# The first sequence of a convolution and mixture-of-experts kernel, convolved in blocks of 112 consecutive tokens by TensorE with tap matrices

## The chip, the cores and the metric

The kernel runs on one core of a Trainium2 chip. The metric is the device time of one launch in microseconds (us); each time quoted is the median of the runs of a kernel, and each figure from a trace is of its one profiled execution.

PE is TensorE's matmuls, PEld its weight loads, DVE VectorE, ACT ScalarE, POOL GpSimd, SP the queue that issues most loads. In a profile line, `L207` is a line of that kernel's source, and the line numbers shift between kernels: the output scaling on DVE is L772 in the kernel before and L862 in the changed one, the convolution step L207 and L346.

## The reference, cut to what matters

```python
# lightweight convolution: x (8, 3584, 192), 8 heads of 24 channels, 7 taps, causal
w = exp(w - max(w)); w = w / (sum(w) + 1e-9)
out[b, s, h*24:(h+1)*24] = sum_k w[h, k] * x_pad[b, s + k, h*24:(h+1)*24]
# mixture of experts on that: 8 experts of 192 -> 1024 -> 192
for b in range(B):
    prev_e = -1
    for s in range(S):
        fresh_e = argmax(logits[b, s])
        e = fresh_e if s == 0 or local_gate[b, s] < 0.5 else prev_e   # locality gate
        prev_e = e
        out[b, s] = softmax(logits[b, s])[e] * (relu(x[b, s] @ w1[e]) @ w2[e])
```

Each token's expert may depend on the token before it, so the router (the step that picks a token's expert) is a scan along the sequence.

## The kernel before

The tokens are worked in 16 groups of 1792 (two per sequence). A group is convolved, its logits and its router give every token a slot of its expert, POOL scatters the rows to these slots, and blocks of 128 or 256 full slots go through the experts. The first 35 blocks have one unit of 128 rows, then come 87 of two units and 20 of one. Blocks 0 to 6 need rows of group 0 alone, 7 (0-based) and on also those of group 1, 21 and on those of group 2; the first three of two units, 35 to 37, need group 3, and 38 and on group 4. Output scalings are counted below in units from 0: units 0 to 34 are the blocks 0 to 34, and unit 37 is the first of block 36. Groups 0 and 1 are sequence 0: nothing can hide them, as no expert has a row yet.

In the kernel before, a partition holds 14 consecutive tokens, and the load has 128 rows:

```python
def load_x(g):
    x_sb = xs.tile([P, NX, D], F32, name="x_sb")           # 128 x (14 + 6) x 192
    win = bass.AP(tensor=src.tensor, offset=..., ap=[[NT * D, P], [1, NX * D]])
    nc.sync.dma_start(out=x_sb.rearrange("p t d -> p (t d)"), in_=win)
```

Four of group 0's heads go to PE with diagonal matrices, seven matmuls each; the other four to DVE, one first tap and six steps each. From group 2 on all eight heads are on DVE, 48 steps per group, with the first taps on ACT:

```python
for k in range(1, KC):
    nc.vector.scalar_tensor_tensor(cols(h), chans(h, k), c[:, h, k:k + 1],
                                   cols(h), Alu.mult, Alu.add)
    yield 0.6
```

Once experts run, each block lets DVE do a quota of that work, measured in rough microseconds, ahead of the scaling of its own output:

```python
for i, (_, n, _, _) in enumerate(blocks):
    ensure(i)                          # rows; waits until the group of a block is routed
    weights(i + AHEAD)
    hT = hidden(n, wbs[i], xT)
    ...
    step(2.5 if n == 1 else 4.2)
    output(n, wbs.pop(i), xgs.pop(i), hT)      # calls step(1.2) ahead of its scaling on DVE
    step(1.3 if n == 1 else 3.0)
```

With 0.6 charged per convolution step, a one-unit block does 10 of them. The order of instructions on each engine is that of the program (no scheduler moves them).

## Time and profile before

| | before |
|---|---|
| first timing, median (range) | 1382.17 us (1381.35 to 1384.19, 3 runs) |
| the profiled execution | 1367.91 us, span of the core 1366.1 |
| PE busy, share of the span | 97% |
| first expert matmul | 71.64 us |
| output scaling of block 1 on DVE | 88.02 us |
| pace of blocks 1 to 34 | 6.17 us |

The second line is 14 us below the first.

The busy line of the page gives, per engine, busy us, share of the span and instructions; the slices give the share of each fortieth (34 us) in tenths:

```profile
PE 1327.2 (97%) x17142; PEld 1252.3 (92%) x17142; DVE 795.1 (58%) x2459; ACT 512.1 (37%) x1146; POOL 481.2 (35%) x513
...
PE   6789999999999999999999999999999999999998
```

PE is full but for the first three slices. What a change of the first sequence can win lies there. How to read the rest is shown in the prediction below: windows first (which stage has an engine that is not full), then the timeline of that stage (which instruction waits for what).

### The profile page before, as it was taken

What the parts mean: (1) busy time and instruction counts of PE and PEld (TensorE: products, weight loads), DVE (VectorE), ACT (ScalarE), POOL (GpSimd) and SP (SyncE); (2) the same over time, 40 slices, a digit from 0 to 9 for tenths busy, and PEclk for the clock granted to TensorE, in tenths of its full rate; (3) what the DMA queues carried; (4) which work ended last, traced back from release to release, by engine and by line L of the source; (5) the groups of instructions that cost most, each with busy time, mean ns of one, the idle gap of its engine ahead of it and who ended that gap; (6) DMA issues with size and microseconds to landing.
All of it is one profiled execution on the core that took longest, in us unless ns stands there. A gap on an engine that the chain in (4) does not pass through costs nothing. (4 is left out here: it accounts for less than half of the span.)

```text
span 1366.1 us, 41871 instructions
## 1 busy us (share of the span) xinstructions
PE 1327.2 (97%) x17142; PEld 1252.3 (92%) x17142; DVE 795.1 (58%) x2459; ACT 512.1 (37%) x1146; POOL 481.2 (35%) x513
## 2 busy tenths in 40 slices
PE   6789999999999999999999999999999999999998
PEld 4488999999999999999999999999999999999997
DVE  6778999988878777878686868684500000000000
ACT  3243444434333333333343434333333333333333
POOL 1442444434343434344444344443343111112111
PEclk9989999999999999999999999999999999999999
DMA  4399999996675757676767676565566555556893
GB/s 181 102 375 374 374 390 373 359 353 251 235 273 206 267 208 265 213 264 219 264 228 265 223 266 220 208 211 208 212 221 224 202 196 181 181 178 235 318 325 131
DMA packets 65812, 340.75 MB, mean 249 GB/s; under 512 B 12369, under 2 KB 23240, under 8 KB 45395
## 3 DMA queue, kind: packets, MB, share of 16 engines
q1 hardware_dynamic: 43488, 285.35, 57.8%
q0 software_dynamic: 22128, 52.70, 10.2%
q8 instruction: 136, 2.23, 0.7%
q14 instruction: 58, 0.47, 0.1%
q10 hardware_dynamic: 2, 0.00, 0.0%
HBM read 285.20 MB, written 53.29 MB: 248 GB/s over the span
## 5 line engine op out<-in xcount | busy, mean ns | idle before, releaser
L760 PE MATMUL yps<-wb,hT 64*128 64x192 f32 x7328 | 636.9, 325 | 3.7 <-DVE o_sb L772 2.0
L744 PE MATMUL hps<-xT,wb 64*128 64x256 f32 (+1 forms) x6816 | 630.4, 337 | 0.8 <-ACT xT L730 0.6
L760 PEld LDWEIGHTS yps<-wb,hT 64*128 64x128 f32 x7328 | 599.7, 187 | 8.5 <-issue 4.5
L744 PEld LDWEIGHTS hps<-xT,wb 64*128 64x128 f32 x6816 | 567.1, 188 | 41.5 <-issue 1.1
L776 POOL DMA_INDIRECT out_dram<-o_sb,xg x229 | 231.5, 1011 | 664.3 <-DVE o_sb L772 591.6
L207 DVE SCALAR_TENSOR_TENSOR y_sb<-x_sb,c,y_sb 128x336 f32<-128x336 f32 x720 | 406.2, 573 | 28.5 <-ACT y_sb L182 9.3
L749 ACT ACTIVATE hT<-hps 128x512 f32<-128x512 f32 (+1 forms) x568 | 261.3, 512 | 361.2 <-PE hps L744 361.0
L772 DVE SCALAR_TENSOR_TENSOR o_sb<-yps,xg,o_sb 128x192 f32<-128x192 f32 x229 | 87.2, 412 | 488.6 <-ACT o_sb L768 488.6
L567 POOL DMA_INDIRECT slots<-y_sb,posi x224 | 222.7, 994 | 185.7 <-ACT hT L749 92.2
L768 ACT ACTIVATE o_sb<-yps,xg 128x192 f32<-128x192 f32 x229 | 87.0, 419 | 420.6 <-PE yps L760 417.0
L730 ACT COPY xT<-xps 128x768 f32<-128x768 f32 (+1 forms) x142 | 96.7, 681 | 11.6 <-PE xps L279 11.6
L279 PEld LDWEIGHTS xps<-ident,xg 64*128 64x128 f32 x1374 | 71.2, 140 | 13.8 <-issue 3.9
L279 PE MATMUL xps<-ident,xg 64*128 64x64 f32 x1374 | 72.5, 222 | 5.8 <-DMA xg<-slots 5.8
L182 ACT ACTIVATE y_sb<-x_sb,c 128x336 f32<-128x336 f32 x116 | 66.7, 586 | 0.0
L341 DVE STREAM_TRANSPOSE z<-y_sb 128x768 f32<-128x768 f32 (+1 forms) x56 | 45.5, 853 | 0.5
L367 DVE COPY lt<-lq 32x36 f32<-32x36 f32 x224 | 41.6, 186 | 3.5
L351 PE MATMUL hps<-z,wg 64*32 64x128 f32 x1344 | 26.7, 274 | 1.4 <-DVE z L341 1.3
L351 PEld LDWEIGHTS hps<-z,wg 64*32 64x32 f32 x1344 | 20.7, 105 | 5.0 <-DVE z L341 3.0
L190 PE MATMUL hps<-x_sb,wb 128*128 128x336 f32 x56 | 18.9, 506 | 4.0 <-DMA x_sb<-in_x_dram 4.0
L190 PEld LDWEIGHTS hps<-x_sb,wb 128*128 128x128 f32 x56 | 12.1, 218 | 10.5 <-issue 6.2
L190 PE MATMUL yps<-x_sb,wb 128*128 128x336 f32 x56 | 16.8, 451 | 0.0
L190 PEld LDWEIGHTS yps<-x_sb,wb 128*128 128x128 f32 x56 | 10.3, 190 | 4.5
(165 smaller groups left out, 336.0 us busy)
## 6 DMA issues: line engine op xcount, KB each, us to landing
wb<-in_w_dram SPq DMA_DIRECT2D x142, 1536.0 KB
x_sb<-in_x_dram SPq DMA_DIRECT2D x16, 1920.0 KB
xg<-slots SPq DMA_DIRECT2D x87, 258.0 KB
xg<-slots SPq DMA_DIRECT2D x55, 129.0 KB
out_dram<-o_sb,xg POOLq DMA_INDIRECT x229
slots<-y_sb,posi POOLq DMA_INDIRECT x224
wg<-in_wgl_dram SPq DMA_DIRECT2D x1, 144.0 KB
slots<-pad SPq DMA_DIRECT2D x1, 129.0 KB
```

Of the source, the lines that this page charges most:

```text
L182: nc.scalar.activation(cols(h), chans(h, 0), Act.Copy, scale=c[:, h, 0:1])
L190: nc.tensor.matmul(acc, lhsT=dg_of(i, k), rhs=chans(h, k), start=(k == 0), stop=(k == KC - 1))
L207: nc.vector.scalar_tensor_tensor(cols(h), chans(h, k), c[:, h, k:k + 1], cols(h), Alu.mult, Alu.add)
L279: nc.tensor.transpose(to, src[rows], identity=ident[rows, rows])
L567: ins = nc.gpsimd.indirect_dma_start(out=slots[:, :], in_=rows, in_offset=None, out_offset=bass.IndirectOffsetOnAxis(ap=to, axis=0)).ins
L730: copied = nc.scalar.copy(to, at)
L744: nc.tensor.matmul(hps[half][:, j, w], lhsT=wb[rows, f0:f0 + P], rhs=xT[rows, d, w], start=(d == 0 and j == 0), stop=(d == KD - 1), skip_g ...
L749: relu = nc.scalar.activation(hT[:, m:m + 2, w], hps[half][:, :, w], Act.Relu)
L760: nc.tensor.matmul(yps[half][:, k * D:(k + 1) * D], lhsT=hT[rows, m, k * P:(k + 1) * P], rhs=wb[rows, WA + m * D:WA + (m + 1) * D], start= ...
L768: nc.scalar.activation(o_sb[:, k, :], y[k][0], Act.Copy, scale=xg[:, k, 0:1])
L772: nc.vector.scalar_tensor_tensor(o_sb[:, k, :], y[k][1], xg[:, k, 0:1], o_sb[:, k, :], Alu.mult, Alu.add)
L776: sent = nc.gpsimd.indirect_dma_start(out=out, in_=o_sb[:, k, :], in_offset=None, out_offset=bass.IndirectOffsetOnAxis(ap=xg.bitcast(I32)[ ...
```

## The change

Its intent: each group of sequence 0 becomes 16 blocks of 112 consecutive tokens, a token per partition, with the six tokens before them: 118 rows. One matmul then convolves one head of eight blocks with a banded matrix of taps (118 x 112), 16 matmuls per group in place of 28 matmuls and 28 DVE operations in group 0, and the loads are contiguous. The logits are computed from these blocks, and the router's scan runs along 16 rows. Because sequence 0 then needs little of DVE, the change also brings work forward, ahead of the first expert block: ten scatters of group 1 in place of four, and `step(15)`, convolution steps of group 2.

```diff
+NB = 16
+TB = PT // NB            # 112 tokens
+NI = TB + HALO           # 118 rows
+NH = NB // 2
@@ loads @@
+    def load_b(g):
+        x_sb = xs.tile([P, NX, D], F32, name="x_sb")
+        xv = x_sb.rearrange("p t d -> p (t d)")[:NI, :NB * D].rearrange("p (b d) -> p b d", d=D)
+        for b in (slice(0, NH), slice(NH, NB)):
+            nc.sync.dma_start(out=xv[:, b, :], in_=xb[g, :, b, :])
+        return xv
...
-        x_in = {0: load_x(0)}
+        nc.scalar.dma_start(out=hank[:NI], in_=wh)
+        x_in = {0: load_b(0)}
...
+        x_in[1] = load_b(1)
@@ convolution of sequence 0 @@
-    for gen in reversed(conv(0, x_in.pop(0), ON_PE, True)):
-        for _ in gen:
-            pass
+    def wide_conv(g, xv, y_sb, yr, both):
+        for b0 in (0, NH):
+            for h in range(H):
+                ps = hps_p.tile([P, 512], F32, name="hps")[:TB, :NH * GS]
+                nc.tensor.matmul(ps, lhsT=hank[:NI, h, :],
+                                 rhs=xv[:, b0:b0 + NH, h * GS:(h + 1) * GS],
+                                 start=True, stop=True)
...                             # leaves through ACT, in group 0 through DVE in turn
@@ order of the first sequence @@
+    conv1 = wide_conv(1, x_in.pop(1), yb, rest(zb), False)
+    for i, _ in enumerate(wide_route(0, ya, acc[0])):
+        for _ in range([6, 5, 5, 0][i]):
+            next(conv1, None)
...
+    for _ in wide_route(1, yb, acc[1]):
+        step(1.2)
+    for _ in range(10):
+        put()
+    step(15)
```

Not shown: the logits and the router of the first sequence (`wide_logits`, `wide_route`), whose parts the prediction counts, and the host's layouts of x and of the taps, which copy and fill but do no arithmetic.

## The prediction

> **What bounds the kernel now.** I read the table of busy time by windows first, to see in which stage TensorE (PE) is not full:
>
> ```profile
> 0.00:70.00 70.00, 47.81 (x280) 30.14 (x280) 49.97 (x159) 21.57 (x53) 20.03 (x52) 0.94 0.39 140
> 100.00:200.00 100.00, 95.67 (x1590) 92.98 (x1588) 92.45 (x295) 42.23 (x118) 38.10 (x38) 1.00 0.98 380
> 600.00:800.00 200.00, 200.00 (x2524) 188.87 (x2522) 153.10 (x470) 77.86 (x159) 81.88 (x81) 1.00 0.68 243
> ```
>
> Columns: window, length, busy us of PE, weight loads, VectorE (DVE), ScalarE (ACT), GpSimd (POOL), PE clock, DMA share, GB/s. From 400 us on PE is always busy: it is the bound, and the change leaves it alone. The change lives in the first 70 us, a chain before any expert runs. The timeline gives its links:
>
> ```profile
> 8.56 0.40 DVE L180 TENSOR_SCALAR y_sb<-x_sb,c 128x336 f32<-128x336 f32 x1 [2.04 <-DMA x_sb<-in_x_dram]
> ...
> 36.53 0.27 DVE L377 TENSOR_REDUCE mx<-lt 128x14 f32<-128x112 f32 x1
> ...
> 46.56 0.17 DVE L539 CAST posi<-pos 128x14 int32<-128x14 f32 x1
> ...
> 47.67 1.27 POOL L567 DMA_INDIRECT slots<-y_sb,posi  x1 [18.58 <-issue]
> ...
> 64.61 0.96 POOL L567 DMA_INDIRECT slots<-y_sb,posi  x1 [0.30 <-issue]
> ...
> 68.41 1.19 SPq L697 DMA_DIRECT2D xg<-slots  x2
> ...
> 71.64 4.79 PEld L744 LDWEIGHTS hps<-xT,wb 64*128 64x128 f32 x48 [0.76 <-ACT xT L730]
> ```
>
> So: group 0's x at 8.6, logits at 36.5, slots at 46.7, 14 scatters on POOL (one per 1.27 us) to 65.6, rows back, first expert matmul at 71.64. A second bound follows. DVE's timeline once experts run:
>
> ```profile
> 88.02 0.42 DVE L772 SCALAR_TENSOR_TENSOR o_sb<-yps,xg,o_sb 128x192 f32<-128x192 f32 x1 [1.88 <-ACT o_sb L768]
> 88.36 5.84 DVE L207 SCALAR_TENSOR_TENSOR y_sb<-x_sb,c,y_sb 128x336 f32<-128x336 f32 x10
> 94.12 0.41 DVE L772 SCALAR_TENSOR_TENSOR o_sb<-yps,xg,o_sb 128x192 f32<-128x192 f32 x1
> ```
>
> Each one-unit block queues ten convolution steps (5.8 us) and one output scaling (0.4 us) on DVE: 6.1 us. PE needs 5.51 us (its timeline has L744 starting at 87.37 and 92.89). From block 1's L772 (88.02) to block 34's (291.72) it is 203.7 us, 6.17 per block: DVE paces the 35 one-unit blocks. Afterwards two-unit blocks come every 10.8 us on PE. So what counts is **when DVE reaches block 1's scaling**.
>
> **What the Trainium skill says.** (1) "DMA: Bandwidth & Descriptors", section "Why a DMA increments its semaphore by 16 and not by 1": a transfer issued from SP or ACT uses the largest number of DMA engines, up to 16, that divides the outer dimension; 128 partitions get 16, 100 get 10, 127 one. The trace before cannot confirm it: its large loads all have 128 partitions (423 GB/s in 5 to 10 us, so an estimated 26.4 GB/s per engine). (2) "Trainium Kernel Development and Optimization", "Key Constraints": the SP and ACT queues share the same 16 engines. Not shown here either. (3) "TensorE: Matmul & The Clock Gate", Part 1: PE starts at half rate until it has been busy some microseconds. The trace agrees: the convolution's first passes start every 0.56 us up to 14.4 us, then the timeline merges 45 passes into 12.67 us, 0.28 each. (4) Same page, "Step-by-step": matmuls stay in program order. Relevant because the change puts group 1's matmuls ahead of group 0's router on PE.
>
> **The change, part by part.**
>
> *Loads.* Before: 128 rows of 15,360 B (1.97 MB). After: 118 rows (112 tokens and 6 of halo), two transfers of 0.725 MB per group, and tap matrices of 118 rows (0.423 MB) on ACT's queue. 118 = 2 x 59, so by (1) every one of them runs on **two engines, the same two**: 52.9 GB/s instead of 423. From about 2 us (the small weight load landed at 2.05): taps and group 0's x, 1.87 MB, take 35.4 us, to 37; group 1's halves land at 51 and 65. Were they on 16 engines, x of group 0 would be there at about 7.
>
> *Convolution.* Removed: 28 matmuls (18.9 us), 24 DVE steps and 4 first taps (15.9 us), 28 diagonal builds. Added: 16 matmuls of 192 columns. At 0.56 us per cold pass of 336 columns, a pass of 192 costs 0.32, a matmul (two passes) 0.64 cold, 0.32 warm; leaving through ACT and DVE in turn at 0.42 (as L768, same width) hides beside that. With x at hand this stage would end at 17 instead of 28. With x at 37 only the second half's eight remain, to 42.3.
>
> *Logits, router.* 24 transposes, six evictions of 448 columns (0.5 to 0.6), products of 1.5 per half, a turn back: I sum 7.3 us against 8.3 before. Logits at 49.7. Router: 1.9 to the change flags, then a turn and scans on 16 rows (2.9), then counts on PE. But PE's order has eleven of group 1's convolution matmuls before the counting matmuls, and the ninth needs group 1's second half: 65. Three cold ones (1.9) and the counts (0.9): 67.6. DVE's last eight operations (2.6): slots at 70.2 against 46.7.
>
> *Scatters.* 16 of 112 rows, not 14 of 128: POOL ends 2 x 1.27 later relative to its start. First at 71.1, last over at 91.5; plus the 6.07 from there to the expert matmul in the trace before: **97.6 against 71.6**.
>
> *DVE ahead of the experts.* Group 1's convolution leaves through ACT alone, done at 72; its logits at 80.3; its router with eight convolution steps of group 2 and the table: 17.5, so 98. The instruction order then puts **33 convolution steps** (18.9) before block 0's scaling, which ends at 117.4; seven more and two transposes (5.9): block 1's scaling starts at 123.2, against 88.02, +35.2. PE needs only 105 for block 0, so DVE decides.
>
> *Given back.* By instruction order DVE is then exactly four blocks ahead: each later block carries the same load as block i+4 did before. But as each block still gets its ten steps, the pace stays 6.1 and the lead buys nothing. Before has one bad interval (blocks 5 to 6, 113.67 to 122.08, 8.4 us, PE waiting for rows of group 1); after would not: -2.3. Four ordinary blocks (24.6) in place of 25.65: -1. Sum: 35.2 - 3.3 = **+32**, about 1414.
>
> **Rivals.**
> A. *The loads do use all engines.* Then slots 0 come at 35.7, first expert matmul at 62.5, nine earlier. The router of group 1 with its table ends at 63 on DVE; 33 steps follow, block 0's scaling ends at 82.3, block 1's starts at 88.5, against 88.02. The nine microseconds vanish in DVE's queue; the -3.3 remains: some 1379. For it: a tuned kernel would hardly keep a load that waits 30 us; against it: the page's rule, given with examples. 15 in 100.
> B. *The early DVE work pays fully* (lead becomes pace, blocks at 5.51 us): up to 33 x 0.6 = 20 us back. Against it: the load per block in the instruction order is unchanged up to block 35. It would make 1394 with two-engine loads.
> C. *Clock.* PE idles through the loads, so more matmuls run cold; 2 to 4 us more in group 1's logits, on DVE's path: 1418. For it: the clock column shows 0.50 in 65 to 75 before, after a sparse stretch.
>
> **Range and chances.** Main line 1414, plus or minus 8; rival A at 1379, 15 in 100. I put the time at 1412, a little below the main line for B, and the range from 1380 to 1424, to hold most of A's weight. The 2% limits are 1354.5 and 1409.8: faster 0.01, same 0.38, slower 0.61. (The profiled run before was 1367.91 us against the timed 1382.17; I take the difference as constant.)
>
> **What would show it.** DMA share in the first 35 us near 2/16, about 50 GB/s, instead of 181; PE waiting for x_sb from in_xb_dram until about 37, and within the router until about 65; first scatter at 71, first expert matmul at 97, block 0's output scaling at 117 behind 33 convolution steps; then blocks 6.1 to 6.2 us apart and the same PE-bound stage. The prediction is wrong if x lands before 10 us (then rival A, and the first scatter at 36), if the scatters of 112 rows differ much from 0.96 us, or if the one-unit blocks run at 5.5 us after the lead.

## The result, and the profile after

The changed kernel takes 1435.68 us (median of 4, 1434.69 to 1437.28), the kernel before on the same chip 1381.99 (4 runs). The ratio is 1.0387, 95% interval 1.0369 to 1.0405: slower by nearly 4%. The direction is as predicted; the time lies 12 us above the predicted range and 24 above the predicted value.

The table of busy time by windows, changed kernel. Columns as in the prediction: window, length, busy us of PE, PEld, DVE, ACT, POOL, PE clock, DMA share, GB/s:

```profile
0.00:10.00 10.00, 0.56 (x2) 0.49 (x2) 0.67 (x4) 1.49 (x2) 4.35 (x39) 1.00 0.17 51
10.00:20.00 10.00, 0.00 (x0) 0.00 (x0) 0.00 (x0) 0.00 (x0) 0.00 (x0) 1.00 0.13 53
20.00:30.00 10.00, 0.00 (x0) 0.00 (x0) 0.00 (x0) 1.76 (x7) 0.00 (x0) 1.00 0.13 52
...
50.00:60.00 10.00, 7.25 (x35) 5.34 (x33) 5.74 (x24) 3.31 (x9) 0.00 (x0) 0.83 0.72 214
60.00:70.00 10.00, 0.22 (x2) 0.09 (x1) 0.62 (x4) 1.76 (x4) 0.00 (x0) 0.61 0.13 54
```

All engines stand still from 10 to 28 us and again from 62 to 70, while the DMA engines are busy by 0.13, that is 2 of 16 (0.125), at 52 to 54 GB/s. Between 50 and 60 another load, x of group 2 with 128 rows, runs beside them: 214 GB/s in all. The timelines of PE, then of DVE (start, busy us, engine, line, operation, out<-in, count, and in brackets the wait with its releaser):

```profile
32.27 5.46 PE L179 MATMUL hps<-x_sb,wb 118*112 118x192 f32 x16
39.70 5.43 PE L179 MATMUL hps<-x_sb,wb 118*112 118x192 f32 x16 [1.96 <-DMA x_sb<-in_xb_dram]
...
69.94 2.23 PE L179 MATMUL hps<-x_sb,wb 118*112 118x192 f32 x6 [9.78 <-DMA x_sb<-in_xb_dram]
...
102.03 5.12 PE L834 MATMUL hps<-xT,wb 64*128 64x128 f32 x48 [0.58 <-ACT xT L820]
```

```profile
75.64 0.17 DVE L435 CAST posi<-pos 112x16 int32<-112x16 f32 x1
...
86.82 0.39 DVE L240 COPY wb<-yps 128x224 f32<-128x224 f32 x1 [6.79 <-remote]
90.34 0.31 DVE L245 COPY lt<-yps 112x144 f32<-112x144 f32 x1 [3.13 <-issue]
...
109.37 19.36 DVE L346 SCALAR_TENSOR_TENSOR y_sb<-x_sb,c,y_sb 128x336 f32<-128x336 f32 x33
128.65 0.41 DVE L862 SCALAR_TENSOR_TENSOR o_sb<-yps,xg,o_sb 128x192 f32<-128x192 f32 x1
...
136.10 0.38 DVE L862 SCALAR_TENSOR_TENSOR o_sb<-yps,xg,o_sb 128x192 f32<-128x192 f32 x1
```

The chain is the predicted one. Group 0's second half comes at 39.7; the convolution of group 1 waits for its second half to 69.9 in the middle of group 0's router; the slots are there at 75.6; DVE then ends the router of group 1 at 109.4 and does 33 convolution steps in a row before the first output scaling at 128.65. The two lines at 86.82 and 90.34 were not foreseen: DVE waits 6.8 us for something "remote" and then 3.1 us in a wait marked "issue". These are the profile's words for a wait that ended on a signal to which it finds no instruction, and for a wait in which it sees nothing waited for.

### The profile page after: what moved, and what is told of

It reads as the page before. It is cut to its first block, busy times and chain, and to the rows that moved or that the text cites. A ratio compares the mean times of both kernels' runs of the same rounds, so it can differ in the third digit from the quotient of the medians.

```text
span 1435.6 us, 41650 instructions
## 1 busy us (share of the span) xinstructions
PE 1344.5 (94%) x17048; PEld 1298.1 (90%) x17048; DVE 777.2 (54%) x2420; ACT 515.1 (36%) x1145; POOL 484.8 (34%) x522
## 5 line engine op out<-in xcount | busy, mean ns | idle before, releaser
L834 PE MATMUL hps<-xT,wb 64*128 64x256 f32 (+1 forms) x6816 | 653.6, 340 | 11.5 <-issue 10.0
L850 PE MATMUL yps<-wb,hT 64*128 64x192 f32 x7328 | 649.9, 326 | 6.8 <-issue 2.7
L834 PEld LDWEIGHTS hps<-xT,wb 64*128 64x128 f32 x6816 | 612.8, 190 | 30.1 <-issue 17.8
L850 PEld LDWEIGHTS yps<-wb,hT 64*128 64x128 f32 x7328 | 609.7, 188 | 13.9 <-issue 6.4
L346 DVE SCALAR_TENSOR_TENSOR y_sb<-x_sb,c,y_sb 128x336 f32<-128x336 f32 x672 | 382.5, 580 | 52.5 <-ACT y_sb L338 22.2
L318 PEld LDWEIGHTS xps<-ident,xg 64*128 64x128 f32 x1374 | 81.4, 140 | 3.6 <-DMA xg<-slots 0.3
L318 PE MATMUL xps<-ident,xg 64*128 64x64 f32 x1374 | 80.4, 223 | 0.0
L338 ACT ACTIVATE y_sb<-x_sb,c 128x336 f32<-128x336 f32 x112 | 62.4, 583 | 0.0
L179 PE MATMUL hps<-x_sb,wb 118*112 118x192 f32 x64 | 21.1, 514 | 11.7 <-DMA x_sb<-in_xb_dram 11.7
L179 PEld LDWEIGHTS hps<-x_sb,wb 118*112 118x112 f32 x64 | 18.1, 294 | 13.5 <-issue 12.5
```

Of the source, the lines that this page charges most:

```text
L318: nc.tensor.transpose(to, src[rows], identity=ident[rows, rows])
L338: nc.scalar.activation(cols(h), chans(h, 0), Act.Copy, scale=c[:, h, 0:1])
L834: nc.tensor.matmul(hps[half][:, j, w], lhsT=wb[rows, f0:f0 + P], rhs=xT[rows, d, w], start=(d == 0 and j == 0), stop=(d == KD - 1), skip_g ...
L850: nc.tensor.matmul(yps[half][:, k * D:(k + 1) * D], lhsT=hT[rows, m, k * P:(k + 1) * P], rhs=wb[rows, WA + m * D:WA + (m + 1) * D], start= ...
```

## The experiments

Eighteen runs, in six calls; runs of one call share a chip and its runs of the kernel before. The table sorts them by chip. "Before" is its median there; the difference is of medians.

| run | chip | before | this | difference | ratio (95% interval) |
|---|---|---|---|---|---|
| e0_before | 0 | 1382.66 | 1382.72 | +0.1 | 1.0000 (0.9976 to 1.0025) |
| e1_pad128 | 0 | 1382.66 | 1399.25 | +16.6 | 1.0127 (1.0087 to 1.0166) |
| e3_nostep | 0 | 1382.66 | 1422.45 | +39.8 | 1.0281 (1.0256 to 1.0306) |
| e4_before_two | 0 | 1382.66 | 1416.26 | +33.6 | 1.0239 (1.0213 to 1.0266) |
| e22_pad_short | 0 | 1382.35 | 1388.96 | +6.6 | 1.0047 (1.0035 to 1.0060) |
| e2_pad_nostep | 12 | 1366.61 | 1361.22 | -5.4 | 0.9954 (0.9940 to 0.9967) |
| e7_split | 12 | 1366.61 | 1370.15 | +3.5 | 1.0024 (1.0011 to 1.0038) |
| e9_pad_nostep_short | 12 | 1366.61 | 1364.70 | -1.9 | 0.9977 (0.9964 to 0.9991) |
| e10_before_short | 12 | 1366.61 | 1383.23 | +16.6 | 1.0118 (1.0102 to 1.0133) |
| e12_after_again | 14 | 1367.41 | 1407.81 | +40.4 | 1.0293 (1.0279 to 1.0307) |
| e14_pad_nostep_again | 14 | 1367.41 | 1360.86 | -6.6 | 0.9963 (0.9946 to 0.9980) |
| e11_late_x3 | 14 | 1367.41 | 1364.08 | -3.3 | 0.9976 (0.9961 to 0.9991) |
| e15_before_late_w | 14 | 1367.41 | 1371.35 | +3.9 | 1.0029 (1.0016 to 1.0042) |
| e17_before_late_w_again | 14 | 1367.31 | 1370.60 | +3.3 | 1.0028 (1.0013 to 1.0042) |
| e18_after_late_both | 14 | 1367.31 | 1407.35 | +40.0 | 1.0301 (1.0285 to 1.0317) |
| e19_pad128_again | 14 | 1367.31 | 1369.75 | +2.4 | 1.0017 (1.0003 to 1.0031) |
| e20_before_late_w_3 | 14 | 1367.32 | 1371.04 | +3.7 | 1.0032 (1.0016 to 1.0048) |
| e21_after_late_both_2 | 14 | 1367.32 | 1406.91 | +39.6 | 1.0294 (1.0277 to 1.0310) |

The same kernel before took 1382.66 and 1382.35 on chip 0, and 1366.6 to 1367.4 on the chips 12 and 14. I call chip 0 slow and the other two quick. Compare only differences and ratios between chips, and traces only within one kind.

### A control, which showed the two kinds of chip

> The kernel before, unchanged, for a trace on the same chip as the experiments. Both theories: 1382, within 0.3%. The first profile of it (1366 us of span) lay 14 us under its timed runs; if this trace is again near 1366 the profiled execution is an easy one, if near 1380 the extra time will show as stretches in which PE's matmuls start one by one with 'issue' ahead of them.

The time is that of before, as expected; the extra time was expected ahead of PE's matmuls and shows first at ACT. The trace is not that of the first profile: the span is 1380.9, not 1366.1, and the two part at one place. First ACT in the first profile of before, then SP and ACT in this run:

```profile
56.22 3.03 ACT L308 COPY z<-hps 128x512 f32<-128x512 f32 x6
```

```profile
56.81 0.37 SPq L690 DMA_DIRECT2D wb<-in_w_dram  x1
```

```profile
59.39 0.58 ACT L308 COPY z<-hps 128x512 f32<-128x512 f32 x1 [2.96 <-remote]
60.78 0.58 ACT L308 COPY z<-hps 128x512 f32<-128x512 f32 x1 [0.81 <-remote]
67.94 2.05 ACT L308 COPY z<-hps 128x512 f32<-128x512 f32 x4 [6.57 <-remote]
```

Six copies that take 3.03 us in one execution take from 59.4 to 70.0 in the other, with waits for something "remote". They begin about when the load of the first expert's weights is issued beside the scatters. Summed over the whole trace, ACT waits for "remote" 26.6 us in this run and 0 in the first profile. It is 0 in every trace of the chips 12 and 14, of whichever kernel, and 27.3 to 56.7 in the other traces of chip 0 and in that of the result. So the first profile has the trace of a quick chip, and the first timing and the result (before at 1382) have the time of a slow one. That is inferred; the records do not name those chips. Chip 0 was slow; whether it is the chip itself or something else about its place is not known.

### The two-engine load, measured on the kernel before

```diff
-        nc.sync.dma_start(out=x_sb..., in_=win)
+        for rows in ([slice(0, 118), slice(118, P)] if g == 0 else [slice(0, P)]):
+            nc.sync.dma_start(out=to[rows], in_=win[rows])
```

> The kernel before with only its first x load cut into 118 and 10 rows: same bytes, same layout, same compute. Theory two-engine loads: 118 rows bring 1.81 MB over two engines, so x lands near 37 instead of 8.6 and the whole chain moves: 1382 + 28 = 1410 (1404 to 1416). Rival, two transfers cost one more fixed latency and no more: within 3 us of 1382.

Only the first load is cut, into 118 and 10 rows of the same bytes. Windows of this run, and the first operation of DVE that needs x:

```profile
20.00:30.00 10.00, 0.00 (x0) 0.00 (x0) 0.00 (x0) 0.00 (x0) 0.00 (x0) 1.00 0.12 52
30.00:40.00 10.00, 0.00 (x0) 0.00 (x0) 0.00 (x0) 0.00 (x0) 0.00 (x0) 1.00 0.13 55
```

```profile
42.05 0.40 DVE L182 TENSOR_SCALAR y_sb<-x_sb,c 128x336 f32<-128x336 f32 x1 [35.47 <-DMA x_sb<-in_x_dram]
```

x comes at 42.05 instead of 8.46 in the control on the same chip, 33.6 us later, and the kernel is 33.6 us slower: nothing hides the first load. The share and the rate are those of two engines. The time lies just above the expected 1404 to 1416. The rate is the one estimated (52 to 55 GB/s from 20 to 40 us); the estimate left out that x of group 1 and other loads run beside it in the first 10 us (215 GB/s in all in that window), which may be the cause and was not measured apart.

### The loads repaired

x blocks and tap matrices padded by the host from 118 to 128 rows, the matmuls unchanged (they still read 118):

```diff
-            nc.sync.dma_start(out=xv[:, b, :], in_=xb[g, :, b, :])
+            nc.sync.dma_start(out=full[:, b, :], in_=xb[g, :, b, :])     # 128 rows
-        nc.scalar.dma_start(out=hank[:NI], in_=wh)
+        nc.scalar.dma_start(out=hank, in_=wh)
```

> The changed kernel with its x blocks and tap matrices loaded as 128 rows (10 of them never used), nothing else altered. Theory two-engine loads: x of group 0 lands by 9 us instead of 39.7, slots of group 0 near 37 instead of 75.6, first expert matmul near 63 instead of 102; 1379, between 1372 and 1390, so 45 to 60 us under the changed kernel. Rival, the row count does not matter and the block layout itself is slow: x still lands after 30 us and the time stays above 1420.

On the slow chip this recovers 36.4 of 53.7 us (1435.68 to 1399.25), 20 fewer than expected; the trace has many standstills of the kind above (ACT 54.1 us of "remote"). So it was run on a quick chip too:

> The changed kernel with x and tap matrices padded to 128 rows and nothing else, on whatever chip comes. Slow: ratio 1.0127 as before. Quick: between the padded kernel without the step (0.9954 to 0.9963) plus the step's 9 to 13 us, and the run with 112 + 6 rows (1.0024): 1.000 to 1.006.

There it recovers 38 of 40.4 (differences +2.4 and +40.4). DVE in that trace:

```profile
65.41 19.38 DVE L347 SCALAR_TENSOR_TENSOR y_sb<-x_sb,c,y_sb 128x336 f32<-128x336 f32 x33
84.71 0.41 DVE L863 SCALAR_TENSOR_TENSOR o_sb<-yps,xg,o_sb 128x192 f32<-128x192 f32 x1
...
92.17 0.38 DVE L863 SCALAR_TENSOR_TENSOR o_sb<-yps,xg,o_sb 128x192 f32<-128x192 f32 x1
```

This is the prediction's rival A: it put block 0's scaling at 82.3 (its end), block 1's at 88.5 and the kernel 3 us below before; they are 85.1, 92.2 and 2.4 above.

The third variant leaves the layouts alone and cuts each load of 118 rows into 112 and 6:

```diff
+            for r in (slice(0, TB), slice(TB, NI)):
-            nc.sync.dma_start(out=xv[:, b, :], in_=xb[g, :, b, :])
+                nc.sync.dma_start(out=xv[r, b, :], in_=xb[g, r, b, :])
```

> The changed kernel with its layouts untouched; each load of 118 rows is issued as one of 112 rows and one of 6. If the number of DMA engines is the largest one up to 16 that divides the outer dimension, 112 rows take 16 engines and the 6 rows (5% of the bytes) take 6, so x of group 0 lands before 15 us, DMA share is well over 2/16 in the first 20 us, and the time is near the padded kernel's 1399.3: 1395 to 1408. Rival (only 128 full rows get all engines): x still at over 30 us and 1425 to 1440.

1.0024, level with the padded kernel's 1.0017. So 128 is not the point; 112 = 16 x 7 rows are as good, and the cause is the number 118 = 2 x 59. (The two ran on different chips, both quick.)

### The early convolution steps

```diff
-    step(15)
```

> The changed kernel without the 25 convolution steps that stand on VectorE before block 0 (loads left on 118 rows). Theory DVE order: block 0's output scaling comes near 114 instead of 128.7 and the lead bought nothing, so the time falls by 9 to 15 us, to about 1424. Rival, the lead pays itself back in the one-unit blocks: within 3 us of 1435.7.

13.2 us less than the changed kernel (1422.45 against 1435.68): the time is as expected, the way to it is not. In its trace 7 steps instead of 33 stand before the first scaling, but that comes at 123.04, not near 114, as it then waits for ACT:

```profile
109.44 4.07 DVE L346 SCALAR_TENSOR_TENSOR y_sb<-x_sb,c,y_sb 128x336 f32<-128x336 f32 x7
...
123.04 0.42 DVE L862 SCALAR_TENSOR_TENSOR o_sb<-yps,xg,o_sb 128x192 f32<-128x192 f32 x1 [9.53 <-ACT o_sb L858]
```

At block 1 the gain is 5.5 us (130.60 against 136.10), at unit 34 it is 7.8 and at unit 39 14.6. PE's matmuls of block 1 start one by one with "issue" waits from 112 to 122 us in this trace: a standstill of the slow chip, which the early steps had hidden.

Both repairs together, on two quick chips:

> The changed kernel with both repairs at once: x blocks and tap matrices padded to 128 rows, and no step(15) ahead of the expert loop. If the two costs are separate, the gain of leaving step(15) out (13.2 us without the padding) comes on top of the padded kernel's 1399.3: about 1386, 1380 to 1392, that is level with the kernel before (1382.7). Rival (the early DVE work pays once x comes early, or it hides behind something else in the padded kernel): 1396 to 1402. Block 1's output scaling should then start some 13 us earlier than in the padded kernel.

> Padded and without step(15), once more as the base of the next run and to tie the two chips together: ratio 0.9954 if the chip is of the quick kind (before 1366), 1.000 to 1.008 if it is of the other (before 1382), where the first run of the padded kernel (with the step) stood at 1.0127.

0.9954 and 0.9963. This version beats the kernel before by 0.4 to 0.5% on quick chips (outside the intervals, though under the 2% from which a kernel is called faster). On the same chip 14 the padded kernel with the step is at 1.0017, so the early steps cost 0.54% there (some 7 us; 8.9 by the two medians). It was not run on chip 0.

### Does DVE pace the one-unit blocks?

The quotas of a one-unit block shortened so that it does 8 steps, not 10:

```diff
-        step(2.5 if n == 1 else 4.2)
+        step(2.1 if n == 1 else 4.2)
-        step(1.3 if n == 1 else 3.0)
+        step(1.1 if n == 1 else 3.0)
```

> The kernel before with 8 instead of 10 convolution steps per one-unit block, nothing else. Tests the DVE pacing on the kernel before: if DVE paces, blocks go from about 6.2 to 5.5 us and the time from 1382.7 to 1368 (1360 to 1384, the upper end if the postponed steps come back as a wait of PE for rows of a later group). Rival (DVE doesn't pace): 1382.7 within 3 us.

> As the run with padding and without step(15), and in addition each one-unit block queues 8 convolution steps instead of 10 (about 1.1 us less DVE work per block). If DVE paces these 35 blocks (6.1 to 6.3 us each against 5.5 of PE), the pace falls to about 5.5 and up to 20 us come off; as the work postponed must be done by a deadline, part may come back as a wait for rows: 1372, range 1362 to 1388. Rival (something else, say ACT or the loads, paces them): within 4 us of the run with 10 steps.

Both missed: e10, expected 15 us below the kernel before (1 above it at worst, if PE came to wait), came 16.6 above it, and e9, expected 14 below the run with ten steps, 3.5 above it. Yet the blocks did run faster. DVE in the short-quota kernel before:

```profile
94.90 0.42 DVE L772 SCALAR_TENSOR_TENSOR o_sb<-yps,xg,o_sb 128x192 f32<-128x192 f32 x1 [0.58 <-ACT o_sb L768]
95.23 4.75 DVE L207 SCALAR_TENSOR_TENSOR y_sb<-x_sb,c,y_sb 128x336 f32<-128x336 f32 x8
100.42 0.42 DVE L772 SCALAR_TENSOR_TENSOR o_sb<-yps,xg,o_sb 128x192 f32<-128x192 f32 x1 [0.43 <-ACT o_sb L768]
```

5.52 us apart, DVE waiting for ACT and so for PE: here PE paces. Block 34 came at 279.95 instead of 291.72. Then PE waited for DVE (PE, then POOL in the same run):

```profile
303.30 1.40 PE L351 MATMUL hps<-z,wg 64*32 64x128 f32 x8 [12.85 <-DVE z L341]
...
307.73 5.45 PE L744 MATMUL hps<-xT,wb 64*128 64x256 f32 x48
```

```profile
294.37 0.96 POOL L567 DMA_INDIRECT slots<-y_sb,posi  x1 [0.30 <-DVE y_sb L207]
...
302.87 0.96 POOL L567 DMA_INDIRECT slots<-y_sb,posi  x1 [0.31 <-issue]
```

L351 are logits, L744 the first matmuls of block 36, which start without a wait: its rows (group 3) were there. DVE had written the slots of groups 3 and 4 at 206.5 and 266.5, and those of group 5 follow at 330.2, so these are the logits of group 5, whose convolution DVE had put off. What puts them ahead of block 36 is the loop in `ensure`: two blocks ahead of the first that needs group 4 (block 38), all scatters of group 4 must be out, and for each that is missing it queues `step(4.2)`, 4.2 us of DVE's work by the quota. Here seven of the 14 were missing (POOL, 294.37 to 302.87), 29.4 us by the quota; in the kernel before none was, the last went out at 282.6. Unit 37 was at 330.65 against 312.27: 11.8 us gained up to block 34, some 30 lost after. In the padded kernel without the step, short quotas gain 11.7 us up to block 34 (276.60 against 288.32) and lose 14.0 to unit 37 (310.93 against 308.68); there four scatters were missing, 16.8 us by the quota. So behind DVE's pace in the one-unit blocks stands **a deadline: DVE's work up to the scatters of group 4** (the recorded text of e22 says group 3). Less per block only moves the work behind it, and the loop then brings more forward than is missing. This is read from the program and two traces; no run changed the loop.

If that is right, steps done early are worth something as soon as the quota lets blocks use them. Last run: padded, `step(15)` kept, quotas short.

> The padded kernel with step(15) kept, and 8 instead of 10 convolution steps per one-unit block. If DVE's total work up to the first block with rows of group 3 is what bounds the one-unit blocks, the 25 steps done early (14 us) fill most of the wait that the run with padding, without the step and with 8 steps met there (block 34 to 37: 34 us in place of 20): block 1's scaling near 92, block 34's near 278, block 37's near 299 instead of 311, and the ratio on a quick chip about 0.990, 0.986 to 0.996. Rival (the lead is lost anyway): the wait at block 35 stays, ratio 1.002 to 1.008.

It met the slow chip, so its ratio compares with the padded kernel's there: 1.0047 against 1.0127, 10.3 us less by the medians. From block 34 to unit 37 it takes 23.9 us (296.11 to 320.05), not 34.3 as in the run without the early steps (20.8 in the kernel before on the slow chip): the last scatter of group 4 went out at 294.6, and the wait is gone. So much of the mechanism held; the ratio expected for a quick chip was not tested, and what the early steps are worth in time under short quotas wasn't either, as no run with short quotas and without them met a slow chip. On this chip it does not beat the kernel before.

### The changed kernel on a quick chip

> The changed kernel once more, unchanged, because chips differ: the kernel before took 1382.7 on the chip of the first four experiments and 1366.6 on that of the second four. If the chips differ by stalls that every version meets alike, the ratio stays 1.0387: within 0.5% of it. If a chip without stalls in the router of group 1 is met (before at 1366), the changed kernel loses its stalls there (5 to 12 us between 84 and 99 us of the trace) too: ratio 1.031 to 1.040. On a chip with before at 1382: 1433 to 1438.

1.0293: below the range that I had put on either kind of chip. The first output scalings on DVE:

```profile
101.26 19.42 DVE L346 SCALAR_TENSOR_TENSOR y_sb<-x_sb,c,y_sb 128x336 f32<-128x336 f32 x33
120.60 0.41 DVE L862 SCALAR_TENSOR_TENSOR o_sb<-yps,xg,o_sb 128x192 f32<-128x192 f32 x1
...
128.04 0.38 DVE L862 SCALAR_TENSOR_TENSOR o_sb<-yps,xg,o_sb 128x192 f32<-128x192 f32 x1
```

Against the result's trace (109.37, 128.65, 136.10) the router of group 1 ends 8.1 us earlier here, without any "remote" wait.

### Do large loads cause the standstills of the slow chip?

Loads taken out of the stretch where they occur, in three ways: x of group 3 later (e11, on the padded kernel without the step), the first weights issued behind the first two blocks' rows (e15, on the kernel before), both (e18, on the changed kernel).

```diff
 # e15, and in e18 with x_in[3] = load_x(3) moved to block 0
-    weights(0)
     for j in range(2):
         xgs[j] = load_rows(j)
+    weights(0)
```

> As the run above, but the load of group 3's x (1.97 MB) is issued at block 1 instead of during the router of group 1. If the stalls of PE, ACT and DVE in the router of group 1 come from large loads that run beside the scatters, a third to a half of the large traffic goes from that stretch: on a chip of the slow kind 3 to 8 us less than the run above, on a quick one nothing there (within 3 us). Rival (stalls come from something else): no difference on either kind of chip.

> The kernel before with one reordering on the SP queue: the first expert's weights are loaded behind the first two blocks' rows, not ahead of them, so that no large load runs beside the scatters of group 0 and the router of group 1 (48 to 68 us). In the trace of the kernel before that was taken on the slow kind of chip, ACT stood still there for 10 us, from the issue of that load (56.8) on. If the load causes it: on a slow chip 5 to 10 us less than before (the weights then come some 3 us later than the rows), on a quick chip 0 to 4 us more. Rival (the load isn't the cause): 2 to 5 us more on both.

> The same as the run before_late_w, in the hope of a slow chip (before at 1382). There, if the load of the first weights beside the scatters causes the standstill: 5 to 10 us less than before. On a quick chip 4 us more, as measured. Rival (not the cause): 2 to 5 us more on a slow chip too.

> The changed kernel with both large loads taken out of the stretch in which the router of group 1 runs: x of group 3 is loaded at block 0, and the first weights behind the first two blocks' rows. On a slow chip, if these loads cause the standstills there: 5 to 12 us less than the changed kernel, that is a ratio of 1.030 to 1.035. On a quick chip the ratio stays at 1.029 to 1.034 (nothing to save; the first weights come 3 us later, but DVE's queue of 33 steps hides that). Rival: 1.0387 on a slow chip.

> The kernel before with the first weights loaded behind the first rows. On a slow chip 5 to 10 us less than before if that load causes the standstill, 2 to 5 us more if not; on a quick chip 4 us more, as measured twice.

> The changed kernel with both large loads late. On a slow chip a ratio of 1.030 to 1.035 if the loads cause the standstills, 1.0387 if not; on a quick chip 1.030, as measured.

All three calls met quick chips. There the results are those expected where there is nothing to save: 1.0028 to 1.0032 for late weights before (PE waits for them, line below), 1.0301 and 1.0294 for both in the changed kernel; e11 is 3.2 us above the run without its edit (1364.08 against 1360.86), where within 3 was expected. The wait summary of PE, e15:

```profile
PE hps L744 <- DMA wb<-in_w_dram: 6.7, 2, 6.4
```

(us in total, times, longest.) Whether these loads cause the standstills on a slow chip is **left open**: no such kernel met one.

## Why the prediction was wrong, and where it was right

Its own steps, against a pair of quick traces (e12 over the first profile) and a pair of slow ones (the result over e0), all in us:

| step | predicted | quick | slow |
|---|---|---|---|
| second half of group 0's x | 37 | 39.4 | 39.7 |
| second half of group 1's x | 65 | 69.9 | 69.9 |
| slots of group 0 | 70.2 | 75.6 | 75.6 |
| first expert matmul | 97.6 | 102.9 | 102.0 |
| router of group 1 and table done on DVE | 98 | 101.3 | 109.4 |
| the 33 convolution steps | 18.9 | 19.4 | 19.4 |
| scaling of block 1 | 123.2 | 128.0 | 136.1 |
| block 1, less that of before | +35.2 | +40.0 | +38.7 |
| unit 6, less before | | +36.6 | +38.4 |
| unit 34, less before | | +37.5 | +41.3 |
| last unit, less before | +32 | +35.4 | +54.2 |

**Right: the mechanism, link by link.** Two DMA engines at the estimated rate (share 0.13, 52 to 54 GB/s, and e4 and e7 for the cause), a wait for group 1's x inside group 0's router, DVE's queue of 33 steps as what decides, and the give-back: on the quick pair 3.4 us come back from block 1 to block 6 (+40.0 to +36.6), where the prediction had 3.3 in all. It put the sum at +32; the quick pair of traces has +35.4 at the last unit.

**Mis-sized: what runs beside the loads.** Group 1's second half came at 69.9, not 65. The prediction's 3.32 MB (taps and four halves) in the 67.9 us from 2 us on are 49 GB/s, where it had taken two engines at 26.4, 52.9. The rate was right where the two engines had these loads alone (52 to 54 GB/s in the windows from 10 to 30, 40 to 50 and 60 to 70); but the prediction counted no other load. In the first 5 us the gate's weights are loaded too, and from 50 to 60 x of group 2, when the window has 214 GB/s in all and, by the packets in the trace, a row of a half takes 0.27 to 0.36 us on its engine instead of 0.24. Its 37 for the first group was 2.4 early, for the first reason in part. By DVE's own times 3.3 us of this reach the end of group 1's router (101.3, not 98); with 0.5 in the 33 steps, and two transposes and seven steps between blocks 0 and 1 that took 7.0 (121.0 to 128.0) and not 5.9, this gives the 4.8 us by which block 1 is late.

**The step that failed: the base.** The prediction says in brackets: "The profiled run before was 1367.91 us against the timed 1382.17; I take the difference as constant." It is not constant: the profile has a quick chip's trace, the timing a slow chip's time, and the slow chip takes more from the changed kernel than from the one before. By the medians the change costs 40.4 us on a quick chip and 53.7 on the slow one. Put the other way, the difference that was taken as a constant 14.3 us is about 15 for the kernel before (1382.66 against 1367.41) and 27.9 for the changed one (1435.68 against 1407.81). 13.3 of the 21.7 us between the main line (1414) and the result are that. A further 3.4 is what the quick pair of traces shows over the main line (+35.4 against +32): the loads and the transposes, less a little more given back. The remaining 5.0 is for the most part the spread of runs: the profiled run of the changed kernel on the quick chip, 1403.68, is the fastest of its five (median 1407.81).

What the slow chip takes is seen in the sums of ACT's "remote" waits: 26.6 us in the kernel before, 56.7 in the changed one, 54.1 padded, 54.4 without the step; 0 for each that was traced on a quick chip. In the result's trace they do not lie in the chain of sequence 0 alone. ACT in block 0 of the changed kernel, where DVE's 33 steps hide the wait (the scaling comes at 128.65):

```profile
122.40 0.42 ACT L858 ACTIVATE o_sb<-yps,xg 128x192 f32<-128x192 f32 x1 [10.57 <-remote]
```

and PE around 370 us, where the logits of a later group go out in handfuls with waits without a releaser:

```profile
370.58 0.44 PE L463 MATMUL hps<-z,wg 64*32 64x128 f32 x4 [0.34 <-issue]
371.34 0.42 PE L463 MATMUL hps<-z,wg 64*32 64x128 f32 x5 [0.32 <-issue]
```

The slow pair's difference grows by 6.8 us from unit 34 to unit 39 (+41.3 to +48.1) and by 4.5 more to unit 121 (+52.6), while the quick pair's rises by 0.7 (+37.5 to +38.2) and then falls to +35.7. So the prediction's "the change leaves it alone", said of PE from 400 us on, did not hold on the slow chip: of the 18.8 us by which the slow pair ends above the quick one, 3.8 are there at unit 34, 9.9 at unit 39 (386 us) and 16.9 at unit 121. All 23 of ACT's "remote" waits in the result's trace are for tiles that PE writes (`xps`, `hps`, `yps`). DVE's at 86.82 ends 2.7 us after PE's last matmul into its tile is recorded as over (84.07); on the quick chip DVE follows after 0.04 us (82.97, 83.01). So the chain seems to stop on PE's side. Why, and why the sum of these waits is twice as large in the changed kernel, is not known. PE, ACT and DVE stop together while large loads and scatters fill the DMA engines, and the trace shows the queues that bring instructions (q8 and q14, 2.7 MB in the run) on the same engines; that late instructions are the cause is argued from this, not shown.

**Rivals.** A (all engines used) was wrong for the kernel as it is, but is what the padded kernel does: 1.0017 on a quick chip against a predicted 0.998. B (the early work pays) was wrong as the quotas stand: on a quick chip the 26 steps cost 8.9 us by the medians (e14, e19). With shorter quotas the wait behind block 34 goes (e22); what that is worth was not measured. The prediction's reason, "as each block still gets its ten steps, the pace stays 6.1 and the lead buys nothing", was therefore right, but the view that DVE's pace is a bound of its own was not: e9 and e10 show the deadline of group 4's scatters behind it. C (the clock) was not tested by a run; the granted clock of the changed kernel on the quick chip was 0.982 over its span, against 0.994 in the first profile, and the steps above leave it little to explain there.

**The range** of 1380 to 1424 was stretched downwards for a rival that did not come about, and had no room for a difference between chips. On a quick chip the kernel takes 1407.81, which lies within it by luck: from that chip's base of 1367.41 the predicted +32 would be 1399.

## What to carry to other kernels

Before a tile shape is chosen for the sake of the matmul, look at the outer number of rows of its loads: 118 rows took two DMA engines of 16 and cost 38 us of 40 on a quick chip, and 112 + 6 rows or padding to 128 gave them back. Work moved to the front of an in-order queue delays what stands behind it (here 26 steps, 8.9 us of the time on a quick chip), and cannot pay later if each block behind it still brings as much work as before; and where a quota "paces" a stage, look for the deadline behind it before cutting it. When a profile and a timing of the same kernel differ by 1%, find out why before predicting a change from them: here the two had come, by all signs, from two kinds of chip.

## What the Trainium skill lacked or had wrong

The first two points are rules that held; the other two are what no page was found to say.

- "DMA: Bandwidth & Descriptors", section "Why a DMA increments its semaphore by 16 and not by 1": the rule on the number of engines held (118 rows: DMA share 0.12 to 0.13; 112 + 6 rows as fast as 128), and it was what made the direction predictable. With nothing beside them, two engines moved 52 to 54 GB/s, which is two shares of the 26.4 estimated from 423 GB/s on 16.
- "Trainium Kernel Development and Optimization", section "Key Constraints": that the queues of SP and ACT share the engines was seen: taps on ACT's queue and x on SP's together stayed at 51 to 53 GB/s, and the taps landed only at 28.2 us (8.6 when padded).
- No page that I found says that chips differ for one kernel, by how much, or how to see it: 1382.7 and 1366.6 to 1367.4 us for the kernel before, with 26.6 us of ACT waits for "remote" in the trace on one kind and none on the other, and 13 us more between the two kernels.
- No page that I found tells how to trace waits that this profile gives as "remote" or, on several engines at once, as "issue" to their cause; one of them took 10.57 us.
